# Batch 2's q in two pieces, from the maxima to the DMA transpose, with the attention matmuls in the order of the pieces

## The chip, the cores and the metric

The kernel runs on one core of a Trainium2 chip. The metric is device time in microseconds (us), the median of several executions. Five engines of the core work side by side and meet only at semaphores: TensorE (PE, matmuls; its weight loads are listed as PEld), VectorE (DVE), ScalarE (ACT), GpSimd (POOL), and SyncE (SP), which here only issues DMA transfers. Each engine runs its own instructions in the order in which the program gives them, so an instruction that waits holds up all that stand behind it on its engine.

## The reference

Two layers, one after the other: a linear attention and a feed-forward layer with a leaky ReLU. Softmax is taken of q over its 64 features and of k over the 576 positions.

```python
# q, k, v: (8, 8, 576, 64) = batch, head, position, feature; float32
q_s = exp(q - max(q, -1)); q_s = q_s / (sum(q_s, -1) + 1e-9)
k_s = exp(k - max(k, 2));  k_s = k_s / (sum(k_s, 2) + 1e-9)
kv  = einsum('bhsd,bhse->bhde', k_s, v)
a   = einsum('bhsd,bhde->bhse', q_s, kv)
x   = a.transpose(0, 2, 1, 3).reshape(4608, 512)   # tokens x model
h   = x @ w_in                                      # (512, 2048)
out = maximum(0.01 * h, h) @ w_out                  # (2048, 512)
```

## The kernel before

**Data.** A batch's q, k or v is one tile of 128 partitions x 4 x 9 x 64 float32: 128 partitions are two heads of 64 position groups, the 4 (HL) are pairs of heads, the 9 (R) are the positions in a group, called rows here, and 64 are the features. So a whole q is 128x2304, five of its rows 128x1280, four 128x1024.

**Attention of one batch.** For k: a tree of maxima (k_tree, L155 to L160, VectorE), the maximum over positions (k_allmax, L165 to L185), the subtraction (k_sub, L193), the exponential (k_exp, L201, ScalarE). For v: a cast to bf16 (v_cast, L213, GpSimd). For q: maxima over features (q_max, L224, VectorE), subtraction (q_sub, L229, GpSimd), exponential (q_exp, L237, ScalarE), sum and reciprocal (q_sum, L246 and L248, VectorE), multiplication (q_norm, L253, VectorE, in place in the bf16 tile qe). From batch 2 on, q_turn (L403, L404) transposes the whole of qe into qX by one DMA that SyncE issues; batches 0 and 1 transpose on TensorE instead. kv (L268) makes the 64x64 products on TensorE, kd_make (L283, L286) scales them on VectorE into the block-diagonal weights kd. attend_x (L411) multiplies kd with qX, for one of four head pairs g and one piece of rows at a time, and ScalarE copies the result to xT (L417), the transposed input of the feed-forward layer. The pieces XR are rows 0 to 4 (320 tokens) and 5 to 8 (256 tokens), so there are eight such matmuls in a batch.

**Feed-forward layer.** The 4608 tokens are taken in nine tiles of 512 (t = 0 to 8). For each, layer 1 (layer1, L423) fills 16 PSUM tiles ph, each from four matmuls over xT in the order g = 0, 2, 1, 3; ScalarE applies the leaky ReLU (leaky, L432) into gj. Then layer 2 (layer2, L444) goes through four row tiles of 128 tokens, 16 matmuls each, into PSUM tiles pout; each is copied (store, L438) and written out by two DMAs (L441) that SyncE issues.

**The order.** The schedule is written out by hand. The function at(t, u, ...) hangs a batch's steps on a place in the feed-forward layer of token tile t: u = 0 to 15 is after the u-th tile of layer 1, u = 16 + 4 s + c is after the c-th group of four matmuls of row tile s in layer 2. What hangs on a place is put into the engines' queues there, in the order in which it was hung. plan2 (L575 to L587) hangs batch 2's steps into token tile 1; plan (L557) does it for batches 3 to 7 and isn't touched. Token tile 2 holds tokens 1024 to 1535, and batch 2 begins at token 1152: its layer 1 needs all eight of batch 2's attention results but for the last tokens. A later batch's loads hang on u = 2 of a token tile (L555); SyncE issues loads, transposes and stores in program order. In token tile 1 the copies of the first two row tiles are ScalarE's, the others VectorE's (L638).

PSUM has six rotating tiles for ph, the kv products and the attention results, and two for pout.

Of the kernel before, what the change touches and what calls it, by code (L numbers as in the profile page):

```python
# [9 lines left out]
BF16 = mybir.dt.bfloat16  # L10
# [10 lines left out]
R = 9  # L21
# [4 lines left out]
def kernel(  # L26
# [9 lines left out]
    nc = tc.nc  # L36
# [10 lines left out]
    P = 128  # L47
# [15 lines left out]
    qT_pool = ctx.enter_context(tc.tile_pool(name="qT", bufs=2))  # L63
# [8 lines left out]
    def load(src, b, name, cuts):  # L72
# [12 lines left out]
    ALLH, ALLR = slice(0, HL), slice(0, R)  # L85
    RA, RB = slice(0, 4), slice(4, R)
    st = [{} for _ in range(B)]
# [7 lines left out]
        out=st[0]["q"][:, :, RB].rearrange("p h r d -> p h (r d)"),  # L95
        in_=qflat[:, :, RB].rearrange("p h r d -> p h (r d)"),
# [48 lines left out]
    def k_begin(b):  # L145
        st[b]["ke"] = ke_pool.tile([P, R, HL, D], BF16, name="ke")
        st[b]["kmax"] = mx_pool.tile([P, HL, D], FP32, name="kmax")
        st[b]["kmaxT"] = mx_pool.tile([P, HL * D], FP32, name="kmaxT")
        st[b]["kall"] = mx_pool.tile([P, HL, D], FP32, name="kall")

    def k_tree(b, hs):
        n = hs.stop - hs.start
        ks = st[b]["k"][:, hs]
        t4 = mx_pool.tile([P, HL, 4, D], FP32, name="t4")[:, 0:n]
        nc.vector.tensor_tensor(out=t4, in0=ks[:, :, 0:4], in1=ks[:, :, 4:8], op=ALU.max)  # L155
        t2 = t4[:, :, 0:2]
        nc.vector.tensor_tensor(out=t2, in0=t2, in1=t4[:, :, 2:4], op=ALU.max)  # L157
        t1 = t4[:, :, 0]
        nc.vector.tensor_tensor(out=t1, in0=t1, in1=t4[:, :, 1], op=ALU.max)  # L159
        nc.vector.tensor_tensor(out=st[b]["kmax"][:, hs], in0=t1, in1=ks[:, :, 8], op=ALU.max)  # L160

    def k_allmax(b):


        nc.vector.transpose(  # L165
            out=st[b]["kmaxT"], in_=st[b]["kmax"].rearrange("p h d -> p (h d)")
        )
        m2 = small_pool.tile([P, CB, 2], FP32, name="m2")
        nc.vector.tensor_reduce(
            out=m2[:, :, 0],  # L170
            in_=st[b]["kmaxT"].rearrange("p (c j) -> p c j", j=32),
            axis=AX.X,
            op=ALU.max,
        )
        for a in range(4):
            o = a ^ 1
            nc.vector.tensor_reduce(
                out=m2[32 * o : 32 * o + 32, :, 1],
                in_=m2[32 * a : 32 * a + 32, :, 0:1],
                axis=AX.X,  # L180
                op=ALU.max,
            )
        m = small_pool.tile([P, CB], FP32, name="m")
        nc.vector.tensor_reduce(out=m, in_=m2, axis=AX.X, op=ALU.max)
        nc.vector.transpose(  # L185
            out=st[b]["kall"].rearrange("p h d -> p (h d)"),
            in_=m.unsqueeze(2).to_broadcast([P, CB, 32]),
        )

    def k_sub(eng, b, hs):  # L190
        ks = st[b]["k"][:, hs]
        n = hs.stop - hs.start
        eng.tensor_tensor(  # L193
            out=ks,
            in0=ks,
            in1=st[b]["kall"][:, hs].unsqueeze(2).to_broadcast([P, n, R, D]),
            op=ALU.subtract,
        )

    def k_exp(b, hs):  # L200
        nc.scalar.activation(  # L201
            out=st[b]["ke"][:, :, hs].rearrange("p r h d -> p h r d"),
            in_=st[b]["k"][:, hs],
            func=AF.Exp,
        )

    def v_cast(eng, b, gg):
        o = vb2[b % 2][:, :, gg, 0:128].rearrange("p r (h d) -> p h r d", h=2)
        i = st[b]["v"][:, 2 * gg : 2 * gg + 2]
        if eng is nc.scalar:  # L210
            eng.copy(out=o, in_=i)  # L211
        else:
            eng.tensor_copy(out=o, in_=i)  # L213


    def q_begin(b):
        st[b]["qe"] = qe_pool.tile([P, R, HL, D], BF16, name="qe")
        if b < 2:
            st[b]["qT"] = qT_pool.tile([P, NB, R, L], BF16, name="qT", tag="qT")

    def q_max(b, rs):
        n = rs.stop - rs.start
        st[b]["qmax", rs.start] = m = small_pool.tile([P, HL, n], FP32, name="qmax")
        nc.vector.tensor_reduce(out=m, in_=st[b]["q"][:, :, rs], axis=AX.X, op=ALU.max)  # L224

    def q_sub(eng, b, rs):
        n = rs.stop - rs.start
        qs = st[b]["q"][:, :, rs]
        eng.tensor_tensor(  # L229
            out=qs,  # L230
            in0=qs,
            in1=st[b]["qmax", rs.start].unsqueeze(3).to_broadcast([P, HL, n, D]),
            op=ALU.subtract,
        )

    def q_exp(b, rs):
        nc.scalar.activation(  # L237
            out=st[b]["qe"][:, rs].rearrange("p r h d -> p h r d"),
            in_=st[b]["q"][:, :, rs],
            func=AF.Exp,  # L240
        )

    def q_sum(b, rs):
        n = rs.stop - rs.start
        qsum = small_pool.tile([P, n, HL], FP32, name="qsum")
        nc.vector.reduce_sum(out=qsum, in_=st[b]["qe"][:, rs], axis=AX.X)  # L246
        st[b]["qrec", rs.start] = qrec = small_pool.tile([P, n, HL], FP32, name="qrec")
        nc.vector.reciprocal(out=qrec, in_=qsum)  # L248

    def q_norm(b, rs):  # L250
        n = rs.stop - rs.start
        qes = st[b]["qe"][:, rs]
        nc.vector.tensor_tensor(  # L253
            out=qes,
            in0=qes,
            in1=st[b]["qrec", rs.start].unsqueeze(3).to_broadcast([P, n, HL, D]),
            op=ALU.mult,
        )


    def kv(b):

        pkv = [psB_pool.tile([P, 2, 130], FP32, name="pkv", tag=BANK_TAG) for _ in range(2)]
        for gg in range(2):
            for r in range(R):
                for hh in range(2):
                    rows = slice(hh * L, (hh + 1) * L)
                    nc.tensor.matmul(  # L268
                        pkv[hh][:, gg, 0:129],
                        lhsT=st[b]["ke"][rows, r, 2 * gg : 2 * gg + 2].rearrange(  # L270
                            "p h d -> p (h d)"
                        ),
                        rhs=vb2[b % 2][rows, r, gg, 0:129],
                        start=(r == 0),
                        stop=(r == R - 1),
                    )
        st[b]["pkv"] = pkv
# [121 lines left out]
            eng.tensor_copy(out=o, in_=ps)  # L399


    def q_turn(b):
        st[b]["qX"] = qX = qT_pool.tile([P, R * 2, P], BF16, name="qX", tag="qT")  # L403
        nc.sync.dma_start_transpose(out=qX, in_=st[b]["qe"].rearrange("p r h d -> p (r h d)"))  # L404

    def attend_x(b, g, rs, eng):
        hh, gg = divmod(g, 2)
        n = (rs.stop - rs.start) * L
        ps = psB_pool.tile([P, n], FP32, name="po", tag=BANK_TAG)
        qX = st[b]["qX"].rearrange("c (r g) (h l) -> c g h r l", g=2, h=2)  # L410
        nc.tensor.matmul(  # L411
            ps.rearrange("p (r l) -> p r l", l=L), lhsT=kd2[b % 2][:, g], rhs=qX[:, gg, hh, rs]
        )
        c0 = b * S + rs.start * L
        o = xT[:, g, c0 : c0 + n]
        if eng is nc.scalar:
            eng.copy(out=o, in_=ps)  # L417
        else:
            eng.tensor_copy(out=o, in_=ps)
# [35 lines left out]
    def at(t, u, *fns):  # L455
        while t > 0 and u >= 32:
            t, u = t + 1, u - 32
        hooks.setdefault((t, u), []).extend(fns)
# [94 lines left out]
    XR = (slice(0, 5), slice(5, R))  # L553
# [21 lines left out]
    def plan2():  # L575
        b = 2
        at(1, 0, lambda: k_begin(b), lambda: q_begin(b), lambda: k_tree(b, ALLH))
        at(1, 3, lambda: k_allmax(b))
        at(1, 6, lambda: k_sub(nc.vector, b, H0), lambda: k_sub(nc.vector, b, H1))
        at(1, 9, lambda: k_exp(b, ALLH), lambda: q_max(b, ALLR), lambda: q_sub(nc.gpsimd, b, ALLR))  # L580
        at(1, 13, lambda: v_cast(nc.gpsimd, b, 0), lambda: v_cast(nc.gpsimd, b, 1))
        at(1, 16, lambda: q_exp(b, ALLR), lambda: q_sum(b, ALLR), lambda: q_norm(b, ALLR))
        at(1, 21, lambda: kv(b))
        at(1, 22, lambda: kd_make(b))
        at(1, 17, lambda: q_turn(b))
        for i in range(8):
            at(1, 28 + i // 2, lambda i=i: attend_x(b, i // 2, XR[i % 2], nc.scalar))  # L587

    plan2()
    for b in range(3, B):  # L590
        plan(b, {3: 27, 4: 22}.get(b, 17))
# [80 lines left out]
```

## Time and profile before

| what | value |
|---|---|
| median of 3 runs | 299.92 us (299.77 to 300.16) |
| profiled execution | 299.45 us |
| its span, first to last instruction | 297.6 us |
| mean granted TensorE clock | 0.981 |
| PE busy | 284.0 us (95%) |
| VectorE, ScalarE, GpSimd busy | 149.9, 144.6, 89.0 us |
| DMA transposes (L404) | 6, landing 4.5 to 6.5 us after issue |
| token tile 1, from its layer 1 to that of token tile 2 | 58.0 to 88.7 us |

Times in the profile are us from the start of the span; durations of single instructions in the listings of forms are ns. A line of the timeline gives the start, the time it covers, the engine, the kernel's line, the operation, output and input, how many instructions are merged in it, and in brackets the idle time of that engine just before and what ended it. A line of the chain of waits gives start, time and what the end of the kernel hung on then. Matmuls are pipelined: one starts before the one ahead has ended, so the distance from start to start is what one costs.

### The profile page before, as it was taken

To read this page: it belongs to the slowest core of one execution; us is meant where nothing else is said; L and a number is where in the kernel's file an instruction comes from. 1 tells how busy PE (TensorE), PEld (TensorE's weight loads), DVE (VectorE), ACT (ScalarE), POOL (GpSimd) and SP (SyncE) were. 2 spreads that over 40 slices of the span, in tenths; PEclk is the share of its full clock that TensorE was granted. 3 is DMA by queue.
4 is the path that set the end of the run, shared out by engine and by line. 5 is a ranking of instruction groups with operands and counts; after the bars stand their busy time and mean duration, and the time that the engine had idled before them with its cause. 6 is when DMAs were issued, how large, how long until landed. Compare 5 with 4: busy or idle time off the path is not lost.

```text
span 297.6 us, 4221 instructions
## 1 busy us (share of the span) xinstructions
PE 284.0 (95%) x1654; PEld 140.0 (47%) x1654; DVE 149.9 (50%) x232; ACT 144.6 (49%) x236; POOL 89.0 (30%) x60
## 2 busy tenths in 40 slices
PE   7398999999999999999999999999999999999994
PEld 2147855444544455454445444444454444444443
DVE  3996868691974299079548354835450100110011
ACT  1146675569137903881585428542854066016400
POOL 5926082008009504900950094009400000000000
PEclk9669999999999999999999999999999999999999
DMA  7999999397087735775379137933141310131032
GB/s 260 308 225 374 233 199 393 71 286 266 8 180 227 286 71 114 234 280 112 78 238 352 39 70 219 328 80 70 37 79 35 73 35 0 37 72 33 0 73 72
DMA packets 36532, 45.76 MB, mean 154 GB/s; under 512 B 15904, under 2 KB 19232, under 8 KB 36512
## 3 DMA queue, kind: packets, MB, share of 16 engines
q1 hardware_dynamic: 33088, 41.16, 46.8%
q0 software_dynamic: 3264, 4.20, 8.1%
q8 instruction: 13, 0.21, 0.3%
q10 hardware_dynamic: 160, 0.13, 0.1%
q14 instruction: 7, 0.06, 0.1%
HBM read 36.70 MB, written 9.44 MB: 155 GB/s over the span
## 4 chain that ended last, share of the span: by engine, by line
PE 83%; DVE 8%; DMA 3%; ACT 2%; POOL 1%; issue 1%; SPq 0%; POOLq 0%
PE ph L423 39%; PE pout L444 38%; PE pkv L268 3%; PE po L411 2%; DMA k_raw<-in_k_dram 2%; DMA qX<-qe 2%; DVE t L155 1%; POOL k_raw L193 1%; DVE t L157 1%; DVE k_raw L328 1%; ACT vb L211 1%; DVE kmax L160 1%; DVE t L159 1%; ACT xT L397 1%; DVE xT L399 1%
## 5 line engine op out<-in xcount | busy, mean ns | idle before, releaser
L444 PE MATMUL pout<-w_out_sb,gj 128*128 128x512 bf16 (+2 forms) x592 | 130.8, 373 | 0.0
L423 PE MATMUL ph<-xT,w_in_sb 128*128 128x512 bf16 (+1 forms) x640 | 127.4, 358 | 0.7 <-DVE xT L399 0.6
L432 ACT ACTIVATE gj<-ph 128x512 bf16<-128x512 f32 x144 | 82.6, 603 | 58.8 <-PE ph L423 58.1
L423 PEld LDWEIGHTS <-w_in_sb 128*128 128x128 bf16 x640 | 62.2, 98 | 62.8 <-issue 1.9
L444 PEld LDWEIGHTS <-gj 128*128 128x128 bf16 x592 | 56.9, 98 | 61.3
L438 DVE COPY out_sb<-pout 128x512 f32<-128x512 f32 (+1 forms) x34 | 22.7, 675 | 89.2 <-PE pout L444 83.6
L193 POOL TENSOR_TENSOR k_raw<-k_raw,kall 128x2304 f32<-128x2304 f32 (+1 forms) x6 | 29.1, 4843 | 92.0 <-DVE kall L185 76.7
L229 POOL TENSOR_TENSOR q_raw<-q_raw,qmax 128x2304 f32<-128x2304 f32 (+2 forms) x10 | 32.7, 3274 | 29.6 <-DVE qmax L224 24.1
L246 DVE TENSOR_REDUCE qsum<-qe 128x36 f32<-128x2304 bf16 (+2 forms) x10 | 20.7, 2071 | 39.5 <-ACT qe L237 39.5
L417 ACT CAST xT<-po 128x320 bf16<-128x320 f32 (+1 forms) x48 | 16.8, 402 | 33.2 <-PE po L411 33.2
L201 ACT ACTIVATE ke<-k_raw 128x2304 bf16<-128x2304 f32 (+1 forms) x10 | 17.4, 1737 | 24.6 <-POOL k_raw L193 15.6
L224 DVE TENSOR_REDUCE qmax<-q_raw 128x36 f32<-128x2304 f32 (+2 forms) x10 | 20.5, 2061 | 4.9 <-DMA q_raw<-in_q_dram 4.9
L253 DVE TENSOR_TENSOR qe<-qe,qrec 128x2304 bf16<-128x2304 bf16 (+2 forms) x10 | 20.8, 2078 | 0.3
L237 ACT ACTIVATE qe<-q_raw 128x2304 bf16<-128x2304 f32 (+2 forms) x10 | 17.4, 1744 | 6.4 <-POOL q_raw L229 6.4
L213 POOL CAST vb<-v_raw 128x1152 bf16<-128x1152 f32 x14 | 16.0, 1173 | 0.0
L297 PE MATMUL pout<-zero 128*128 128x512 bf16 x24 | 10.8, 631 | 1.3 <-POOL zero L100 1.3
L155 DVE TENSOR_TENSOR t<-k_raw 128x1024 f32<-128x1024 f32 (+1 forms) x10 | 11.7, 1166 | 0.5 <-DMA k_raw<-in_k_dram 0.3
L411 PE MATMUL po<-qX,kd 128*128 128x320 bf16 (+1 forms) x48 | 9.8, 286 | 0.7 <-DMA qX<-qe 0.7
L438 ACT COPY out_sb<-pout 128x512 f32<-128x512 f32 (+1 forms) x3 | 1.6, 549 | 17.3 <-PE pout L444 17.3
L268 PEld LDWEIGHTS <-ke 64*128 64x128 bf16 x252 | 7.2, 93 | 3.3 <-ACT gj L432 1.7
L268 PE MATMUL pkv<-vb,ke 64*128 64x129 bf16 x252 | 8.5, 216 | 0.2 <-ACT vb L211 0.2
L286 DVE TENSOR_TENSOR kd<-pkv,krec 64x128 bf16<-64x128 f32 x28 | 8.1, 289 | 0.7
(51 smaller groups left out, 96.3 us busy)
## 6 DMA issues: line engine op xcount, KB each, us to landing
out_dram<-out_sb SPq DMA_DIRECT2D x70, 128.0 KB, 2.4
q_raw<-in_q_dram SPq DMA_DIRECT2D x7, 1152.0 KB, 8.6
v_raw<-in_v_dram SPq DMA_DIRECT2D x7, 1152.0 KB, 10.9
k_raw<-in_k_dram SPq DMA_DIRECT2D x6, 1152.0 KB, 5.9
k_raw<-in_k_dram SPq DMA_DIRECT2D x4, 576.0 KB, 5.6
w_in_sb<-in_moe_w_in_dram POOLq DMA_DIRECT2D x8, 256.0 KB, 6.1
w_out_sb<-in_moe_w_out_dram POOLq DMA_DIRECT2D x4, 512.0 KB, 13.5
v_raw<-in_v_dram SPq DMA_DIRECT2D x2, 576.0 KB, 7.5
```

The source lines that it names most:

```text
L193: eng.tensor_tensor(out=ks, in0=ks, in1=st[b]["kall"][:, hs].unsqueeze(2).to_broadcast([P, n, R, D]), op=ALU.subtract,)
L201: nc.scalar.activation(out=st[b]["ke"][:, :, hs].rearrange("p r h d -> p h r d"), in_=st[b]["k"][:, hs], func=AF.Exp,)
L224: nc.vector.tensor_reduce(out=m, in_=st[b]["q"][:, :, rs], axis=AX.X, op=ALU.max)
L229: eng.tensor_tensor(out=qs, in0=qs, in1=st[b]["qmax", rs.start].unsqueeze(3).to_broadcast([P, HL, n, D]), op=ALU.subtract,)
L237: nc.scalar.activation(out=st[b]["qe"][:, rs].rearrange("p r h d -> p h r d"), in_=st[b]["q"][:, :, rs], func=AF.Exp,)
L246: nc.vector.reduce_sum(out=qsum, in_=st[b]["qe"][:, rs], axis=AX.X)
L253: nc.vector.tensor_tensor(out=qes, in0=qes, in1=st[b]["qrec", rs.start].unsqueeze(3).to_broadcast([P, n, HL, D]), op=ALU.mult,)
L268: nc.tensor.matmul(pkv[hh][:, gg, 0:129], lhsT=st[b]["ke"][rows, r, 2 * gg : 2 * gg + 2].rearrange("p h d -> p (h d)"), rhs=vb2[b % 2][row ...
L423: nc.tensor.matmul(ph, lhsT=w_in_sb[:, cb, j * P : (j + 1) * P], rhs=xT[:, cb, c0 : c0 + n], start=(i == 0), stop=(i == NB - 1),)
L432: nc.scalar.activation(out=o, in_=ph, func=AF.Prelu, alpha=LEAKY_SLOPE)
L438: copy(out=out_sb, in_=pout)
L444: nc.tensor.matmul(pout, lhsT=g_sb[j // 2][:, j % 2, tsub * P : (tsub + 1) * P], rhs=w_out_sb[:, j, os], start=(j == 0), stop=(j == NF - 1),)
```

## The change

Only batch 2 is touched. q_turn gets a slice of rows and transposes these alone, into their part of qX, which is allocated with the first piece. In plan2 the maxima, the subtraction, the exponential, the sum with its reciprocal, the multiplication and the transpose are issued once for rows 0 to 4 and once for rows 5 to 8:

- both pieces' maxima and subtractions hang on the same place as before (u = 9), piece by piece;
- the first piece's exponential, sum and multiplication hang on u = 13, behind the v casts there, and its transpose on u = 15; those of the second piece on u = 16 and u = 17, where the whole stood before;
- the eight attention matmuls stay at u = 28 to 31, two to a place, but in the order of the pieces: all four g of the first piece, then all four of the second. Before, both pieces of a g stood together.

```diff
-    def q_turn(b):
-        st[b]["qX"] = qX = qT_pool.tile([P, R * 2, P], BF16, name="qX", tag="qT")
-        nc.sync.dma_start_transpose(out=qX, in_=st[b]["qe"].rearrange("p r h d -> p (r h d)"))
+    def q_turn(b, rs=ALLR):
+        if rs.start == 0:
+            st[b]["qX"] = qT_pool.tile([P, R * 2, P], BF16, name="qX", tag="qT")
+        nc.sync.dma_start_transpose(
+            out=st[b]["qX"][:, 2 * rs.start : 2 * rs.stop],
+            in_=st[b]["qe"][:, rs].rearrange("p r h d -> p (r h d)"),
+        )
...
-        at(1, 9, lambda: k_exp(b, ALLH), lambda: q_max(b, ALLR), lambda: q_sub(nc.gpsimd, b, ALLR))
+        at(1, 9, lambda: k_exp(b, ALLH))
+        for rs in XR:
+            at(1, 9, lambda rs=rs: q_max(b, rs), lambda rs=rs: q_sub(nc.gpsimd, b, rs))
         at(1, 13, lambda: v_cast(nc.gpsimd, b, 0), lambda: v_cast(nc.gpsimd, b, 1))
-        at(1, 16, lambda: q_exp(b, ALLR), lambda: q_sum(b, ALLR), lambda: q_norm(b, ALLR))
+        for i, rs in enumerate(XR):
+            at(1, (13, 16)[i], lambda rs=rs: q_exp(b, rs), lambda rs=rs: q_sum(b, rs), lambda rs=rs: q_norm(b, rs))
+            at(1, (15, 17)[i], lambda rs=rs: q_turn(b, rs))
         at(1, 21, lambda: kv(b))
         at(1, 22, lambda: kd_make(b))
-        at(1, 17, lambda: q_turn(b))
         for i in range(8):
-            at(1, 28 + i // 2, lambda i=i: attend_x(b, i // 2, XR[i % 2], nc.scalar))
+            at(1, 28 + i // 2, lambda i=i: attend_x(b, i % 4, XR[i // 4], nc.scalar))
```

## The prediction

> **What bounds the kernel now.** The page's first two parts come first: TensorE (PE) is busy for 284.0 of the 297.6 us of the span, and the slices show nines from the second on. So the time is what PE does plus what PE waits for. The list of PE's waits, restricted to 60 us and later, has one row only: a matmul of L411 (the attention matmul) that waits for qX, the DMA transpose of the normalised q, 0.7 us. The timeline of PE shows where:
>
> ```profile
> 82.73 1.67 PE L444 MATMUL pout<-w_out_sb,gj 128*128 128x512 bf16 x7
> 85.09 0.41 PE L411 MATMUL po<-qX,kd 128*128 128x320 bf16 x2 [0.69 <-DMA qX<-qe]
> 85.33 1.02 PE L444 MATMUL pout<-w_out_sb,gj 128*128 128x512 bf16 x4
> ```
>
> Four matmuls of 512 columns take 1.02 us, and one alone shows 0.38, so they start (1.02 - 0.38)/3 = 0.215 apart. The seventh above starts at 82.73 + 6 x 0.216 = 84.03, so the next could have started at 84.24. It starts at 85.09: the loss is 0.85 us, not the 0.69 printed, since the pipeline drained as well. This is batch 2; it is the only batch whose transpose ends a PE wait that the list counts.
>
> The second place is the end of this stage. The chain of waits reads:
>
> ```profile
> 88.58 0.24 PE po L411 x2
> 88.82 0.65 PE ph L423 x3
> 89.47 0.03 issue
> 89.50 13.32 PE ph L423 x61
> ```
>
> The first layer-1 tile of the next stage takes xT in the order g = 0, 2, 1, 3. Its matmuls start at 88.66, 88.87 and 89.09 (single rows of the timeline), the fourth at 89.50 instead of 89.305: 0.195 us lost to the last ScalarE copy, that of g = 3, piece 2, which ends at 89.07 + 0.38 = 89.45.
>
> Then the way to qX, from the timeline:
>
> ```profile
> 65.49 2.54 DVE L224 TENSOR_REDUCE qmax<-q_raw 128x36 f32<-128x2304 f32 x1
> ...
> 67.30 2.12 ACT L201 ACTIVATE ke<-k_raw 128x2304 bf16<-128x2304 f32 x1
> 68.12 4.05 POOL L229 TENSOR_TENSOR q_raw<-q_raw,qmax 128x2304 f32<-128x2304 f32 x1 [21.94 <-DVE qmax L224]
> 69.31 3.27 ACT L432 ACTIVATE gj<-ph 128x512 bf16<-128x512 f32 x6
> ...
> 72.11 2.24 POOL L213 CAST vb<-v_raw 128x1152 bf16<-128x1152 f32 x2
> 72.47 2.12 ACT L237 ACTIVATE qe<-q_raw 128x2304 bf16<-128x2304 f32 x1
> 74.62 2.55 DVE L246 TENSOR_REDUCE qsum<-qe 128x36 f32<-128x2304 bf16 x1 [6.58 <-ACT qe L237]
> ...
> 77.62 2.56 DVE L253 TENSOR_TENSOR qe<-qe,qrec 128x2304 bf16<-128x2304 bf16 x1
> ...
> 80.34 2.82 SPq L404 DMA_TRANSPOSE qX<-qe  x1
> ```
>
> Each step waits for the whole of the one before; the transpose is issued at 80.34 and lands 4.71 later, at 85.05.
>
> **The change, step by step.** Seven instructions are added (a second maximum, subtraction, exponential, sum, reciprocal, multiplication and transpose). Batches 0 and 1 already do q in pieces of 4 and 5 rows (128x1024 and 128x1280), so the forms listing has every duration but the transpose's:
>
> ```profile
> L253 DVE TENSOR_TENSOR qe<-qe,qrec 128x1280 bf16<-128x1280 bf16 x2 | 3.0, 1493 | 0.1
> L246 DVE TENSOR_REDUCE qsum<-qe 128x20 f32<-128x1280 bf16 x2 | 3.0, 1485 | 0.9 <-ACT qe L237 0.8
> L224 DVE TENSOR_REDUCE qmax<-q_raw 128x20 f32<-128x1280 f32 x2 | 3.0, 1477 | 0.0
> ...
> L237 ACT ACTIVATE qe<-q_raw 128x1280 bf16<-128x1280 f32 x2 | 2.5, 1270 | 0.6 <-POOL q_raw L229 0.6
> ```
>
> The same listing gives 2.32 for GpSimd's subtraction of 128x1280 (L229), and for 128x1024 1.22 (L253), 1.21 (L246), 1.22 (L224), 1.05 (L237) and 1.90 (L229); the reciprocals are 0.28 and 0.25.
>
> - VectorE and GpSimd. Maxima 65.49 to 66.97 and on to 68.15; subtractions on GpSimd 67.05 to 69.4 and to 71.2; the v casts, queued behind, 71.2 to 73.4, against 74.35 before. They feed the kv matmuls of 77.06, so they have 3.6 us.
> - ScalarE. The first exponential now stands ahead of the last two leaky copies (j = 14, 15), and GpSimd is 1.8 us ahead of it. ScalarE is behind after the k exponential: its copies start 0.48 apart, the fourth at 70.74. So the first exponential starts at 71.22 and takes 1.27; copies 14 and 15 end at about 73.0 and 73.5, against 72.58 before. PE needs them for the 15th and 16th matmul of layer 2, at 71.78 + 14 x 0.216 = 74.8 and 75.0. That cover is 1.5 us; if it is gone, PE waits one for one. The second exponential runs 73.36 to 74.41.
> - VectorE again. First piece 72.53, sum to 74.02, reciprocal to 74.33, multiplication to 75.85. Second piece in the queue behind it: 75.8, 77.0, 77.3, 78.5. The reciprocals of kv, next in the queue, start at 78.5 and not at 80.10.
> - The two transposes. SyncE issues them at 76.0 and 78.65, both ahead of the store of row tile 0 as now. A piece is not in the trace. Upper bound: the whole one's 4.71 (landings in the six batches 4.5 to 6.5). Lower bound: its share of blocks, 10/18 and 8/18 of 4.71, is 2.6 and 2.1. I take a value between, 3.4 and 3.1, as the issue alone is 2.82 of the 4.71 and should go with the blocks. The first lands at 79.4 (78.6 to 80.7), the second at 81.8 (80.8 to 83.4). PE wants them at 84.24 and, after two groups of 2 x 0.136 + 4 x 0.216, at 86.51. Even the upper bounds leave 3 us. The 0.85 goes. The stores behind them are issued from about 80, not 83.25.
> - The Trainium skill speaks against cutting: DMA: Bandwidth & Descriptors, section Bandwidth, asks to gather transfers to 1 MiB or more, and its fit in the section on the anatomy of one DMA gives each a fixed 2.0 us. An estimate from that fit for 320 KB and 256 KB is 2.8 and 2.6 us against 3.4 for the whole, so 2 us more in all; the row of the whole is 4.71, so the fit is short here. By either, the second piece lands before 84, and the sum would be the same.
> - The attention matmuls: eight, as before, columns unchanged in sum. The order changes the last pair: it is now g = 2 and g = 3 of the second piece (256 columns each), where it was both pieces of g = 3. The next stage's second matmul reads g = 2. On the old clock this copy starts at 88.75 and ends 0.38 later at 89.13; with the 0.05 that lay between copy and matmul before, matmul two starts at 89.18 instead of 88.87, matmul four at 89.18 + 2 x 0.216 = 89.61 (its own copy ends at 89.40). That is 0.11 later than the 89.50 of now. Bounds: 0.195 gained if the copies hid wholly, 0.38 lost if one more copy lay in the way.
> - Downstream. Batch 3's VectorE chain starts at 84.30, behind a copy of row tile 2 that comes before the gap; it doesn't move up. Its k subtraction on GpSimd ends at 94.68, and ScalarE wants the result at 95.65, which becomes 94.9: 0.2 of slack. Its q subtraction ends at 98.68, wanted at 100.04, then 99.3. PE runs from 89.5 on without another counted wait, so the gain stays.
>
> Sum: -0.85 + 0.11 = **-0.74 us**. The profiled execution took 299.45 (297.6 of span, 1.85 around it) and would take 298.71; it lies 0.47 below the median of the runs, 299.92, so the forecast for the median is **299.18**. Its own range is 0.65 to 0.95 off, by the bounds of the stage's end short of their far ends: 298.97 to 299.27.
>
> **Rivals.**
> 1. *The second piece comes late* (slower). If SyncE's queue takes the second transpose only when the first has landed, and each takes the slowest landing of the six, 6.54: 76.0, 82.55, 89.09, against 86.51 wanted. -0.85 + 2.58 + 0.11 = +1.84: 301.76. It makes the kernel slower from a landing of 87.25 on. Against it: the store behind the transpose is issued at 83.25, right after the issue and 1.8 before the landing; the 6.54 stands where loads are in flight, while the DMA share between 72.2 and 77.1 is 0.01.
> 2. *The piece doesn't count by itself* (the change doesn't do what it says): the first matmul waits for both transposes, and these follow each other at 4.71: 80.7, 85.4. -0.85 + 1.2 + 0.11 = +0.46: 300.4. Without the queueing, both are in by 83.4 and nothing is lost. Against it: batch 1's second maximum ran at 40.58, ahead of the first piece's subtraction, so pieces of a tile are told apart.
> 3. *The gain is eaten at the stage's end*: one more copy (0.38) ahead of the new second matmul: -0.36, so 299.56. For it: ScalarE is the last wait there already; against it: GpSimd and VectorE have nothing in it.
>
> **How the numbers follow.** Forecast 0.70, rival 1 0.12, rival 2 0.08, rival 3 0.10. Within 0.2% (0.60 us) is about what a measurement of this kernel can't tell from no change. The forecast is only 0.14 past it, so 0.08 of its 0.70 go to "same". Faster: 0.62. Same: 0.08 + 0.08 + 0.10 = 0.26. Slower: 0.12. The range reaches over rival 3 and to no change, 298.85 to 300.0; rival 1 and most of rival 2 are left out.
>
> **What would show it.** Right: no wait of L411 for qX; two transposes issued near 76.0 and 78.7; the first L411 of this stage right after a matmul of L444; the next stage's second L423 matmul late by some 0.3 and the fourth not. Wrong: a wait at L444 in row tile 0 for gj (ScalarE too late), a wait at the fifth attention matmul (second piece too late), or PE waits after 90 that were not there.

## The result, and the profile after

| | before | changed |
|---|---|---|
| median, 15 runs each, same session | 300.14 us | 298.68 us |
| median of the shorter group (below) | 299.93 us (10 runs) | 298.61 us (12 runs) |
| profiled execution, its span | 299.45, 297.6 us | 298.58, 296.8 us |

The ratio is 0.9944, with a 95% interval of 0.9926 to 0.9962. The runs of every kernel that ran more than once, before as well as changed, fall into two groups whose medians lie 1.2 to 1.9 us apart, so small differences below are taken between the medians of the shorter groups (the runs within 1 us of the fastest). In these the change brings **1.32 us**, where 0.74 was forecast, and the median of all runs, 298.68, lies below the forecast's range of 298.85 to 300.0.

The timeline of PE of the changed kernel, at the place of the old wait (lines after the change are 4 higher: L448 is layer 2, L415 the attention matmul, L427 layer 1, L421 the copy to xT):

```profile
82.80 1.67 PE L448 MATMUL pout<-w_out_sb,gj 128*128 128x512 bf16 x7
84.31 0.43 PE L415 MATMUL po<-qX,kd 128*128 128x320 bf16 x2
84.58 1.03 PE L448 MATMUL pout<-w_out_sb,gj 128*128 128x512 bf16 x4
```

82.80 + 7 x 0.216 = 84.31: the first attention matmul follows without a gap. The 0.85 us are gone. The way to qX, from the timeline of the same kernel:

```profile
65.56 2.61 DVE L224 TENSOR_REDUCE qmax<-q_raw 128x20 f32<-128x1280 f32 x2
...
71.29 1.30 ACT L237 ACTIVATE qe<-q_raw 128x1280 bf16<-128x1280 f32 x1
...
72.45 1.11 ACT L436 ACTIVATE gj<-ph 128x512 bf16<-128x512 f32 x2
...
74.45 1.49 DVE L253 TENSOR_TENSOR qe<-qe,qrec 128x1280 bf16<-128x1280 bf16 x1
...
76.10 4.57 SPq L405 DMA_TRANSPOSE qX<-qe  x2
...
77.39 1.22 DVE L253 TENSOR_TENSOR qe<-qe,qrec 128x1024 bf16<-128x1024 bf16 x1
```

From 71.29 on, each start is within 0.15 us of the one forecast (71.22, 72.4, 74.33, 76.0, 77.3). The landings are less close: the first piece landed at 81.22, where 79.4 was forecast and 80.7 as the latest, the second at 81.98 (81.8). Both are ahead of 84.31. At the stage's end, the chain of waits now runs through a copy:

```profile
87.82 0.12 PE po L415
87.95 0.02 issue
87.97 0.38 ACT xT L421
88.35 0.04 issue
88.39 13.76 PE ph L427 x63
```

That is the copy of g = 2, piece 2. Layer 1's first matmul started at 87.88, and the second, at 88.39, could have at 88.095: 0.298 us lost, against 0.195 before.

Two differences were not in the forecast. One is a wait near 195 us, for batch 6's qX:

```profile
194.04 0.59 PE L448 MATMUL pout<-w_out_sb,gj 128*128 128x512 bf16 x2
195.00 0.42 PE L415 MATMUL po<-qX,kd 128*128 128x320 bf16 x2 [0.37 <-DMA qX<-qe]
```

From 194.04 + 2 x 0.216 = 194.47 to 195.00 it is 0.53 us; in the profile of before the same place lost 0.09, too little for the list of waits. The other is the end. In the timeline of the kernel before, and then of the changed one:

```profile
293.65 0.29 DVE L438 COPY out_sb<-pout 128x128 f32<-128x128 f32 x1 [2.80 <-PE pout L444]
293.97 0.47 SPq L441 DMA_DIRECT2D out_dram<-out_sb  x1
294.19 0.48 ACTq L441 DMA_DIRECT2D out_dram<-out_sb  x1
```

```profile
293.73 0.47 SPq L445 DMA_DIRECT2D out_dram<-out_sb  x1
293.74 0.68 ACTq L445 DMA_DIRECT2D out_dram<-out_sb  x1
```

The last two stores wait for the same VectorE copy, which ends at 293.94 before and at 293.70 after. SyncE issues 0.03 us later in both; ScalarE 0.25 later before, 0.03 after. From the end of the last matmul to the end of the span it is 4.04 us before (293.61 to 297.65) and 3.43 after. What the DMA queues did from 294 us on, before and then changed (the last figure of a store is the time from issue to landing):

```profile
q14 instruction: 1, 0.01, 0.7%
...
out_dram<-out_sb SPq DMA_DIRECT2D x1, 32.0 KB, 2.4
out_dram<-out_sb ACTq DMA_DIRECT2D x1, 32.0 KB, 2.4
```

```profile
out_dram<-out_sb SPq DMA_DIRECT2D x1, 32.0 KB, 1.9
out_dram<-out_sb ACTq DMA_DIRECT2D x1, 32.0 KB, 2.1
```

So SyncE's store takes longer too, though it is issued as early, and before, one packet of an instruction queue (q14) is moved beside the two stores. The pair of profiles then adds up: -0.85 (gap), +0.10 (stage's end), +0.44 (batch 6), -0.61 (end), and 0.07 that the start took longer: -0.85, against spans 0.84 apart.

### The profile page after: what moved, and what is told of

It reads as the page before. It is cut to its first block, busy times and chain, and to the rows that moved or that the text cites. A ratio compares the mean times of both kernels' runs of the same rounds, so it can differ in the third digit from the quotient of the medians.

```text
span 296.8 us, 4229 instructions
## 1 busy us (share of the span) xinstructions
PE 284.1 (96%) x1654; PEld 140.2 (47%) x1654; DVE 150.3 (51%) x236; ACT 144.6 (49%) x237; POOL 89.1 (30%) x61
## 4 chain that ended last, share of the span: by engine, by line
PE 83%; DVE 8%; DMA 4%; ACT 2%; POOL 1%; issue 1%; SPq 0%; POOLq 0%
PE pout L448 39%; PE ph L427 38%; DMA qX<-qe 2%; PE pkv L268 2%; PE po L415 2%; DMA k_raw<-in_k_dram 2%; DVE t L155 1%; POOL k_raw L193 1%; DVE t L157 1%; DVE k_raw L328 1%; ACT vb L211 1%; DVE kmax L160 1%; DVE t L159 1%; ACT xT L397 1%; DVE xT L399 1%
## 5 line engine op out<-in xcount | busy, mean ns | idle before, releaser
L448 PE MATMUL pout<-w_out_sb,gj 128*128 128x512 bf16 (+2 forms) x592 | 130.8, 373 | 0.0
L427 PE MATMUL ph<-xT,w_in_sb 128*128 128x512 bf16 (+1 forms) x640 | 127.4, 358 | 0.8 <-DVE xT L399 0.6
L427 PEld LDWEIGHTS <-w_in_sb 128*128 128x128 bf16 x640 | 62.3, 98 | 62.7 <-issue 2.0
L448 PEld LDWEIGHTS <-gj 128*128 128x128 bf16 x592 | 56.8, 98 | 61.4
L421 ACT CAST xT<-po 128x320 bf16<-128x320 f32 (+1 forms) x48 | 16.8, 402 | 32.8 <-PE po L415 32.8
L415 PE MATMUL po<-qX,kd 128*128 128x320 bf16 (+1 forms) x48 | 9.8, 286 | 0.4 <-DMA qX<-qe 0.4
```

The lines of the kernel that those rows point to most:

```text
L427: nc.tensor.matmul(ph, lhsT=w_in_sb[:, cb, j * P : (j + 1) * P], rhs=xT[:, cb, c0 : c0 + n], start=(i == 0), stop=(i == NB - 1),)
L448: nc.tensor.matmul(pout, lhsT=g_sb[j // 2][:, j % 2, tsub * P : (tsub + 1) * P], rhs=w_out_sb[:, j, os], start=(j == 0), stop=(j == NF - 1),)
```

## The experiments

Times are differences of the medians of the shorter groups to the kernel before on the same chip in the same session; "end" is the time from the last matmul's end to the end of the span in the run's profile.

**The two kernels again.** No edit.

> The kernel before, unchanged, for a second profile and for the spread. Theory A (the end): in the first profile an 8 KB packet of the instruction queue at 295.23 us, 0.42 us long, sat on one DMA engine while the last stores went out, and ScalarE's last DMA issue came 0.2 us late; that follows from the program, so it is here again and the time from the end of the last matmul to the end of the span is 4.0 us as before. Theory B (chance): the end differs from run to run, and here it may be 3.4 us as in the changed kernel's profile. Both: ratio 1.000 within 0.002, a gap of 0.85 us ahead of batch 2's first attention matmul, and 0.2 at the stage's end. Open: the wait for batch 6's qX, 0.09 us in the first profile.

> The changed kernel, unchanged, for a second profile. Theory A: from the end of the last matmul to the end of the span 3.4 us again, no instruction packet in the last 3 us; ratio near 0.9955 (1.3 us off, of which 0.74 at batch 2 and 0.5 to 0.6 at the end). Theory B (chance): the end is anything from 3.4 to 4.0 and the ratio is 0.9975 (0.74 us). Open: the wait for batch 6's qX, 0.53 us in the first profile against 0.09 before; if it goes with the change it is above 0.4 here too.

The kernel before against itself: ratio 1.0012 (0.9989 to 1.0036), 0.0 us. The changed kernel: 0.9957 (0.9937 to 0.9977), -1.44 us. Gap and loss at the stage's end came out the same to 0.01 us (0.853 and 0.195; none and 0.298), and so did the ends: 4.05 and 3.45. The wait for batch 6 did not: 0.60 in the kernel before, 0.29 in the changed one, the other way round than in the first pair. So the end goes with the program and batch 6's wait with the run.

**One more instruction on ScalarE, and one more DMA on SyncE.** Each put alone into the kernel before:

```diff
     nc.scalar.activation(out=warm, in_=ident[:, 0:1], func=AF.Exp)
+    nc.scalar.activation(out=warm, in_=ident[:, 0:1], func=AF.Exp)
```

> The kernel before with the exponential on a 128x1 tile at the start (ScalarE idle there) done twice: ScalarE has one instruction more, as in the changed kernel, and nothing else differs. Theory A (ScalarE's instruction stream reaches its next block at the very end): the end shortens from 4.0 to about 3.4 us, ratio 0.998 (0.5 to 0.6 us off). Theory C (one more DMA on SyncE shifts the completion semaphores) and theory B (chance): ratio 1.000.

```diff
         at(1, 17, lambda: q_turn(b))
+        at(1, 17, lambda: hold_sync(1, w_out_sb[0:1, 11, 0:128]))
```

> The kernel before with one more small DMA (256 bytes inside SBUF) on SyncE right behind batch 2's transpose: the completion semaphores of all later DMAs shift by one, as in the changed kernel. Theory C: the end shortens to about 3.4 us, ratio 0.998. Theories A and B: 1.000.

The extra exponential, which does nothing, gives 0.9977 (0.9959 to 0.9995), -0.50 us, and an end of 3.54 us, with batch 2's gap of 0.85 still there. In its timeline ScalarE's last issue no longer comes late:

```profile
293.68 0.47 SPq L442 DMA_DIRECT2D out_dram<-out_sb  x1
293.68 0.68 ACTq L442 DMA_DIRECT2D out_dram<-out_sb  x1
```

The extra DMA gives 1.0008 (0.9986 to 1.003), -0.11 us, and an end of 3.91 us. Of the three theories, only A (ScalarE's instruction stream) fits both: the completion semaphores (C) are out, and so is chance (B).

**ScalarE's count back in the changed kernel**, by giving one of its copies to VectorE.

```diff
-store(row0, po, nc.scalar.copy if t == 1 and tsub < 2 else nc.vector.tensor_copy)
+store(row0, po, nc.scalar.copy if t == 1 and tsub < 1 else nc.vector.tensor_copy)
```

> The changed kernel with the copy of the second row tile in token tile 1 on VectorE (idle at 80.2 us) and not on ScalarE: ScalarE has as many instructions as in the kernel before. Theory A: the 0.6 us at the end are given back (last matmul to end of the span 4.0 us, an instruction packet some 2 us before the end) and what stays is the 0.74 us of batch 2: ratio 0.9975. Theory B or C: 3.4 us and a ratio near 0.9957, as the changed kernel.

The end is 3.93 us, ScalarE's last issue late again (0.25 after the copy's end at 294.71):

```profile
294.42 0.29 DVE L442 COPY out_sb<-pout 128x128 f32<-128x128 f32 x1 [2.80 <-PE pout L448]
294.74 0.47 SPq L445 DMA_DIRECT2D out_dram<-out_sb  x1
294.96 0.48 ACTq L445 DMA_DIRECT2D out_dram<-out_sb  x1
```

The ratio, 0.9993 with an interval of 0.9972 to 1.0015, holds theory A's 0.9975 (and no change) and not the 0.9957 of the others; the difference is -0.67 us. That is near the forecast's 0.74, seen by itself.

Counting ScalarE's records in the traces (instructions, DMA issues and semaphore waits) puts the kernels in two classes:

```
records   kernels                                            end
325       before, e1, e4, f2, g2                             3.9 to 4.3 us
326, 327  after, e2, e3, f1, f3, f5, g1, h1, h2              3.4 to 3.5 us
```

In the first class a packet of 8 KB on an instruction queue starts 2.3 to 2.4 us ahead of the end (295.2 in the kernel before) and takes 0.3 to 0.5 us, while the last stores are in flight. In the second it stands at 280 to 282. In both it starts 1.0 to 1.3 us after ScalarE came to its 320th record: in the kernel before that is a semaphore wait at 294.14, between its last two DMAs; in the changed kernel it is the last copy (with 326 records, the DMA behind it), which had nothing ahead of it from 279.8 on and waited for PE.

The landings show where the time goes. Each of the two last stores lands in 16 parts. In the first class the sixteenth part comes 0.44 to 0.71 us after the fifteenth, for both stores and in all five profiles; in the second never more than 0.04. In the kernel before, fifteen parts of ScalarE's store are in 2.14 us after the end of VectorE's copy and the last at 2.61; in the changed kernel all are in at 2.09. So of the 0.61 us, the late sixteenth part makes 0.47 and the late issue some 0.05 (2.14 against 2.09); the rest lies behind the landing. One packet in the way of one of the DMA engines would look like this. That it is so, and that the packet fetches ScalarE's instructions, is inferred from these times; that one record more takes 0.5 us off the kernel before, and two less put 0.6 to 0.8 back on the changed one, is shown in both directions.

**The order of the matmuls alone.**

```diff
-at(1, 28 + i // 2, lambda i=i: attend_x(b, i % 4, XR[i // 4], nc.scalar))
+at(1, 28 + i // 2, lambda i=i: attend_x(b, i // 2, XR[i % 2], nc.scalar))
```

> The changed kernel with the eight attention matmuls in the old order (both pieces of a head pair together), all else as changed. By the prediction's step for the stage's end: the next layer 1 loses 0.195 us at its fourth matmul and not 0.30 at its second, so 0.10 us less than the changed kernel. The first piece 2 matmul comes right behind the first piece 1 matmul; piece 2 landed at 82.0, so no wait for qX at batch 2. If the order is needed for the gain, that wait is back.

As expected: no wait for qX at batch 2, and 0.195 us at the stage's end, at the fourth matmul again (the trace lacks the record of the third). One run, 297.75 us. The new order is not needed for the gain; it costs 0.10.

**The transpose alone in two pieces.**

```diff
-        at(1, 9, lambda: k_exp(b, ALLH))
-        for rs in XR:
-            at(1, 9, lambda rs=rs: q_max(b, rs), lambda rs=rs: q_sub(nc.gpsimd, b, rs))
+        at(1, 9, lambda: k_exp(b, ALLH), lambda: q_max(b, ALLR), lambda: q_sub(nc.gpsimd, b, ALLR))
...
+        at(1, 16, lambda: q_exp(b, ALLR), lambda: q_sum(b, ALLR), lambda: q_norm(b, ALLR))
+        at(1, 17, lambda: q_turn(b, XR[0]), lambda: q_turn(b, XR[1]))
```

> One part alone: maxima to multiplication on the whole q as in the kernel before, only the transpose in two pieces, and the new order of the matmuls. Prediction's theory (the chain ahead of the transpose is what counts): the first transpose is issued at 80.2 and lands 3.4 to 5.1 us later, 83.6 to 85.3, against 84.2 wanted; the second is issued behind it, at about 82, and lands by 86. A gap ahead of the first attention matmul of 0 to 1.1 us. Rival (a smaller transpose lands sooner and that is the gain): first landing by 83.6, no gap. ScalarE's count of instructions is that of the kernel before, so the end is 4.0 us by theory A.

Here the rival won. From the timeline of this run, SyncE and PE:

```profile
80.33 2.93 SPq L405 DMA_TRANSPOSE qX<-qe  x2
```

```profile
81.64 2.75 PE L448 MATMUL pout<-w_out_sb,gj 128*128 128x512 bf16 x12
84.23 0.43 PE L415 MATMUL po<-qX,kd 128*128 128x320 bf16 x2
```

The pieces are issued at 80.33 and 81.84 and land 3.61 and 3.25 us later, at 83.94 and 85.08; PE takes them at 84.23 and 86.50 without a gap. One run, 298.42 us. So in this profile the pieces ahead of the transpose are not what removes the wait; they turn the 0.3 us of room ahead of the first attention matmul into 3.1 (81.22 to 84.31 in the changed kernel). That room may be needed: the first piece took 3.6 us here, but 5.1 to 5.3 in three of the eight profiles in which all is in pieces, and with 5.1 PE would have waited 1.2 us here. The expected end of 4.0 us was a miss too: it was 3.46. The kernel has one exponential fewer than the changed one but one semaphore wait more than the kernel before, 326 records, so it is the records that count and not the instructions.

**The matmuls one group earlier.**

```diff
-at(1, 28 + i // 2, lambda i=i: attend_x(b, i % 4, XR[i // 4], nc.scalar))
+at(1, 27 + i // 2, lambda i=i: attend_x(b, i % 4, XR[i // 4], nc.scalar))
```

> The changed kernel with batch 2's attention matmuls one group of four layer-2 matmuls earlier (u = 27 to 30). The first piece is then wanted at 83.3 and the second at 85.5; they landed at 81.2 and 82.0, so no wait. The copies to xT have 0.9 us more before the next layer 1, so its loss of 0.30 goes: 0.3 us faster than the changed kernel, ratio 0.9947. If the loss at the stage's end is not from the copies, no difference to the changed kernel.

0.9951 (0.9933 to 0.997), -1.72 us. The loss at the stage's end is gone, as it should be if it came from the copies to xT. But in the profiled run batch 6's wait had become the longest of all:

```profile
195.55 0.42 PE L415 MATMUL po<-qX,kd 128*128 128x320 bf16 x2 [1.26 <-DMA qX<-qe]
```

The transpose took 7.87 us from issue to landing there. In the profiles with all three of batch 7's loads ahead of it that was 6.4 to 7.9 us; batch 7's own transpose, with no load in flight, took 4.55 to 4.60.

**Batch 7's q and v loaded after batch 6's transpose**, once with the matmuls one group earlier in the changed kernel, once in the kernel before (load_one loads one of the three whole):

```diff
-        at(b - 2, 2, lambda b=b: load_all(b))
+        if b < B - 1:
+            at(b - 2, 2, lambda b=b: load_all(b))
...
+    at(B - 3, 2, lambda: load_one(B - 1, "k", k))
+    at(B - 3, 9, lambda: load_one(B - 1, "q", q), lambda: load_one(B - 1, "v", v))
```

> The changed kernel with batch 2's attention matmuls one group earlier (u = 27 to 30), and with batch 7's q and v loaded after batch 6's transpose (u = 9 of token tile 5, k stays at u = 2). Theory: the wait for batch 6's qX near 195 us (0.09 to 1.4 us in the runs so far) comes from these loads, in flight together with the transpose; without them the transpose lands 4.6 us after issue, as batches 3, 4 and 7 do, and the wait is 0. Against the kernel before: 0.85 + 0.20 at batch 2, 0.6 at the end, 0.1 to 0.6 here: 1.75 to 2.25 us off, ratio 0.9925 to 0.994. Rival (the wait has another cause, or late loads hold up batch 7): a wait for qX at 195 stays, or new waits after 200, and the ratio is 0.995 or more.

> The kernel before with batch 7's q and v loaded after batch 6's transpose, nothing else. Theory: no wait for qX at 195, and 0.1 to 0.6 us off, ratio 0.998 to 0.9997; batch 2's gap of 0.85 stays. The end stays at 4.0 us if ScalarE keeps its 325 instruction records, and is 3.4 if a semaphore wait is added there. Rival: the wait stays.

The first: 0.9942 (0.9922 to 0.9963), -1.87 us. The second: 0.9993 (0.9977 to 1.0009), -0.37 us, end 4.26. Neither waits at 195: the transposes landed 4.91 and 5.07 us after issue, and no new wait came behind. So the wait is the loads'. What it costs the kernel before is not settled: the medians of the shorter groups say 0.4 us, but the interval of the ratio reaches over no change.

**The best version beside the changed kernel**, on one chip. The best version is the changed kernel with both edits above, the matmuls one group earlier and the late loads:

> The changed kernel once more, beside the best version on one chip. By the terms so far (0.75 at batch 2, 0.6 at the end, the wait for batch 6's qX unchanged on the mean): 1.3 to 1.4 us off in the shorter group of runs.

> The best version (attention matmuls at u = 27, late loads of batch 7) on the same chip. By the terms: 0.3 less than the changed kernel at the stage's end and 0.1 to 0.6 less at batch 6: 1.7 to 2.2 us off in the shorter group, 0.4 to 0.9 below the changed kernel. If both terms were chance, it is level with the changed kernel.

The changed kernel: 0.9973 (0.9952 to 0.9995), -1.27 us. The best version: 0.9945 (0.9923 to 0.9968), -1.95 us; its seven runs of the shorter group, 297.48 to 297.73, all lie below the changed kernel's seven, 297.92 to 298.73. The timeline of its PE at batch 6 and at the stage's end:

```profile
193.82 0.38 PE L448 MATMUL pout<-w_out_sb,gj 128*128 128x512 bf16 x1
194.03 0.41 PE L415 MATMUL po<-qX,kd 128*128 128x320 bf16 x2
```

```profile
86.87 1.03 PE L448 MATMUL pout<-w_out_sb,gj 128*128 128x512 bf16 x4
87.74 1.46 PE L427 MATMUL ph<-xT,w_in_sb 128*128 128x512 bf16 x5
```

In both places the matmuls follow each other 0.21 us apart.

## Why the prediction was wrong

The direction was right, and so was the gain at batch 2; a term was missing.

- *"The 0.85 goes"*: right, 0.851, in every changed kernel. The forecast times of the chain held to 0.15 us, ScalarE's cover for layer 2 as well (copies ended at 73.6, wanted at 74.9).
- *"0.11 later"* at the stage's end: right, 0.10, at the second matmul as forecast. Moving the matmuls one group earlier takes all of it away.
- *-0.74*: measured alone, with ScalarE's record count put back, -0.67.
- *The step that failed* is "Downstream ... PE runs from 89.5 on without another counted wait, so the gain stays", and the 1.85 us around the span and the end of the span taken as fixed. The seven added instructions were costed by their durations and by what queues behind them, not by their place in ScalarE's instruction stream. Two records more (one is enough) moved what looks like an instruction fetch from the last stores to 14 us before, worth 0.50 (one more record, in the kernel before) to 0.61 us (the ends of the two profiles). With this term the sum is -1.24 to -1.35; measured were -1.32, and -1.44 and -1.27 in the two repetitions.
- *The same step* also passed over 0.09 us at 195, printed in no list. It is the visible end of a wait of 0 to 1.4 us that comes and goes from run to run with and without the change, so it doesn't explain the miss, but it blurs single profiles by as much as the whole forecast. That the two profiles here differ by 0.84 us, near the 0.74 forecast, is luck: 0.61 gained at the end and 0.44 lost at batch 6 nearly cancel.
- *The bounds of the transpose* (2.6 to 4.71 us for the first piece) were too narrow: it landed after 3.57 to 3.88 us in five profiles, and 5.09 to 5.27 in three; why, stays open. Nothing came of it, as 3 us were to spare. The values taken, 3.4 and 3.1, came close to the 3.6 to 3.9 and 3.3 to 3.5 that were usual. The estimate of 2.8 and 2.6 was short; it is from a fit for DMAs that GpSimd issues, and these are SyncE's.
- *The reason* given for the gain, that the whole chain must be cut, was not needed in the one profile that tried it: cutting the transpose alone removed the gap there, with 0.3 us to spare.
- Of the rivals, the late second piece is out (landed at 81.98, wanted at 86.58). The piece that doesn't count by itself is out by the transpose alone in two pieces: its first matmul ran at 84.23, before the second piece landed at 85.08; in the changed kernel both were in. The eaten gain came only as the 0.10 that the forecast had.

## What to carry to other kernels

Where a gain of a few tenths of a per cent is expected, the end of the kernel is part of the sum: look there for a packet of an instruction queue or a late landing among the last stores, and try a version with one idle instruction more before a change is credited with the time. A wait of 0.1 us that no list shows can be the edge of one that is longer in other runs, so take a second profile before a difference between two is explained. And try the smallest cut first: two transposes in place of one removed, in one profile, a wait that the longer chain of cuts was credited with.

## What the runs showed of the hardware

- **Moving instructions isn't always hidden.** In the five profiles with an 8 KB packet of an instruction queue, 0.3 to 0.5 us long, next to the last stores, the end of the span came 3.9 to 4.3 us after the last matmul; in the nine without, 3.4 to 3.5. The Trainium skill (Runtime: NRT & Kernel Launch, section Instruction fetch mechanics) has the fetch go in 16 KiB blocks, at a cost that is mostly hidden. Here the 13 packets of one instruction queue (by their number PE's) are of 16 KB and those of the other, while the kernel runs, of 8 KB; next to the last stores the cost was not hidden.
- **A transpose is slowed by loads in flight**: 4.55 to 4.60 us alone (batch 7), 6.4 to 7.9 (batch 6) with three loads of 1152 KB issued 7 to 8 us before, and 4.7 to 5.1 (batch 6) with two of the three put behind it.
